# Six batches' queries and keys, transposed ahead of time and kept in DRAM

## Chip, cores, metric

The kernel runs on one core of a Trainium2 chip. The metric is the time on the device of one execution, in microseconds (us). The core's engines work in parallel, each through its own list of instructions in order: PE (TensorE, the matrix engine, which also transposes by a matmul with an identity matrix), DVE (VectorE), ACT (ScalarE), POOL (GpSimd). SP issues nearly all DMA transfers, in order as well. PE writes its results to PSUM, and another engine copies them to SBUF.

## What is computed

Attention over the 32 largest scores of each query, then a Fourier mixing block with a two-layer network. The inputs are float32: q, k and v of 8 batches, 8 heads, 576 tokens, 64 channels.

```python
scores = scale * np.matmul(q, k.transpose(0, 1, 3, 2))
kth = np.partition(scores, -top_k, axis=-1)[..., -top_k:-top_k + 1]
scores = np.where(scores >= kth, scores, -1000000000.0)
attn = np.exp(scores - np.max(scores, axis=-1, keepdims=True))
attn = attn / (np.sum(attn, axis=-1, keepdims=True) + 1e-09)
x = np.matmul(attn, v)                   # then (B, H, S, D) -> (B, S, H*D)
mixed = np.real(np.fft.fft(np.fft.fft(x, axis=1), axis=2))
u = x + mixed
un = (u - mean(u)) / np.sqrt(var(u) + 1e-06)
out = u + np.maximum(un @ w_ch1, 0.0) @ w_ch2
```

## The kernel before

**Work and steps.** Two heads make a pair: 4 pairs a batch, 32 in all. Tokens are cut into four blocks of 128 and a tail of 64. An item is one block of queries of one head (or the tails of both heads together): 9 items a pair, 36 a batch, 288 in all. The main loop at the end of the kernel makes one step per item, and each step appends instructions to every engine's list. The order on each engine is therefore written out by the program: a dictionary `plan` holds functions under a step and a place (`at(step, where, fn)`), and the step runs the places in a fixed order.

**What an item passes through.** PE multiplies q and k (`scores`, L401, L386, and L371 for the tail of the keys), ACT copies the scores to SBUF as S (L404, L393, L375), three steps ahead of DVE. DVE takes the 32 largest by four times MAX8 (L425) with MATCH_REPLACE8 between (L427). POOL makes the bounds nt (L434), ACT the mask (L448), POOL subtracts it (L451), ACT takes the exponential (L459). In the first batch, PE then transposes the probabilities (`transposes`, L527, L538, L542), ACT copies them to PT (L530 and after), and PE multiplies them with v (`attend`, L564). In later batches the transposes go through DRAM planes and a transposing DMA instead (`plane`, L472, L485; `turn`, L506).

**Preparing q and k.** The scores need q and k with the channels on partitions. SP loads them with the tokens on partitions (`load_nat`, `load_half`, `load_tails`), in pieces of 256 bytes a token. `prep` (L308 on PE) transposes five blocks of the pair, with two PSUM buffers of the pool `ps_t`, and ACT copies the result: for q a copy of 512 columns and one of 64 (L316), for k one of 512 (L318) and two for the tail, into a tile of its own, kt (L322). The loop calls it for the next pair, for q in the first step of a pair, for k in the sixth.

**The first batch is special.** In it there is no work of the network yet. Instead, the weights are converted: the inputs hold them as 64-bit floats, 32 chunks are loaded (L187), and ACT (L192, L208, L211, at the place "convert", the first thing of ACT's step), DVE (L200) and POOL (L219, L221) make float32 of them, about one chunk a step up to step 35. In a step of this batch ACT has, in order: the conversions, the exp of the last item, copies of scores, copies of `prep`, copies of PT, and the mask of the present item. PE has: scores, `prep`, the transposes of the last item, the product with v (in four steps of nine), three with 128 columns and one with 192.

**Later batches.** The mixing (`dft_tokens`, `dft_channels`) and the network of a batch (`mlp_units`: L966, L993, L1032, L1163) run on PE while the next batch's items pass. The function `level` spreads those units over the steps by estimated cost; `fixed_cost` gives a step's own PE work, with 0.7 us for each `prep`. After the last item there remain the mixing and the network of the last batch.

Of the kernel before, what the change touches and what calls it, by code (L numbers as in the profile page):

```python
# [9 lines left out]
F32 = mybir.dt.float32  # L10
# [9 lines left out]
P = 128  # L20
TH = 32
# [52 lines left out]
def kernel(  # L74
# [9 lines left out]
    nc = tc.nc  # L84
    B, H, S, D = q.shape
    DM = H * D
# [59 lines left out]
    cc = const.tile([P, 2], F32, name="cc", tag="cc")  # L146
    nat_t = const.tile([P, NC, 2, D], F32, name="nat", tag="nat")

    kt_t = const.tile([P, P], F32, name="kt", tag="kt")

    ftail = const.tile([P, DM + 1], F32, name="ftail", tag="ftail")
    v_t = [const.tile([P, NC, 2, D], F32, name=f"v{i}", tag=f"v{i}") for i in range(2)]

# [68 lines left out]


    nat, qT_of, kT_of, v_of, PT, Ssb, Wk, Wp, M8, Nt = ({} for _ in range(10))
    x_of, o_of, xT_of, rd_of = ({} for _ in range(4))


# [6 lines left out]

    def load_half(dst, src, pair, e, h, queue=None):

        r0 = h * (HS if src is q else 2 * P)
        (queue or nc.sync).dma_start(  # L240
            out=dst[:, 2 * h:2 * h + 2, e, :],
            in_=head_of(src, pair, e)[r0:r0 + 2 * P].rearrange("(t p) d -> p t d", p=P),
        )

    def load_tails(dst, src, pair, queue=None, heads=(0, 1)):
        for e in heads:
            if src is q:
                for h in range(2):
                    (queue or nc.sync).dma_start(
                        out=dst[TH * h:TH * (h + 1), NF, e, :],  # L250
                        in_=head_of(src, pair, e)[HS * h + 2 * P:HS * (h + 1)],
                    )
            else:
                r0 = TAIL * e if src is v else 0
                (queue or nc.sync).dma_start(
                    out=dst[r0:r0 + TAIL, NF, e, :], in_=head_of(src, pair, e)[NF * P:S]
                )

    def load_nat(n, pair):
        if pair < NPAIR:  # L260
            nat[n, pair] = nat_t
            src = q if n == "q" else k
            b, hp = divmod(pair, NPB)
            both = src[b, 2 * hp:2 * hp + 2]
            if n == "k":
                for e in range(2):
                    nc.sync.dma_start(
                        out=nat_t[:, 0:NF, e, :],
                        in_=both[e, 0:NF * P].rearrange("(c p) d -> p c d", p=P),
                    )  # L270
                nc.sync.dma_start(
                    out=nat_t[0:TAIL, NF, :, :], in_=both[:, NF * P:S].rearrange("e r d -> r e d")
                )
                return
            for e in range(2):
                for h in range(2):
                    load_half(nat_t, src, pair, e, h)
            for h in range(2):
                nc.sync.dma_start(
                    out=nat_t[TH * h:TH * (h + 1), NF, :, :],  # L280
                    in_=both[:, HS * h + 2 * P:HS * (h + 1)].rearrange("e r d -> r e d"),
                )

    def load_v(pair):
        if pair < NPAIR:
            v_of[pair] = v_t[pair % 2]
            for e in range(2):
                nc.sync.dma_start(
                    out=v_of[pair][:, 0:NF, e, :],
                    in_=head_of(v, pair, e)[0:NF * P].rearrange("(c p) d -> p c d", p=P),  # L290
                )
            load_tails(v_of[pair], v, pair)

    def prep(n, pair, blocks=((0, NF), (NF, NC))):

        if pair >= NPAIR:
            return 0.0
        src, got_of = nat[n, pair], qT_of if n == "q" else kT_of
        if pair not in got_of:
            got_of[pair] = attp.tile(  # L300
                [P, S if n == "q" else NF * P], F32, name=f"{n}T_{pair}", tag=f"{n}T",
                bufs=2 if n == "q" else 1
            )
        t_sb = got_of[pair]
        for c0, c1 in blocks:
            tp = ps_t.tile([P, 4, P], F32, name=f"tp{n}_{pair}_{c0}", tag="tp")
            for c in range(c0, c1):
                nc.tensor.transpose(  # L308
                    tp[:, c - c0, :], src[:, c, :, :].rearrange("p h d -> p (h d)"), ident
                )  # L310
            if c0 < NF:
                dst, got = t_sb[:, c0 * P:c1 * P], tp.rearrange("p a c -> p (a c)")[:, 0:(c1 - c0) * P]
            else:
                dst, got = t_sb[:, NF * P:], tp[:, 0, 0:TAIL]
            if n == "q":
                nc.scalar.mul(out=dst, in_=got, mul=scale)  # L316
            elif c0 < NF:
                nc.scalar.copy(out=dst, in_=got)  # L318
            else:
                for e in range(2):  # L320
                    r = slice(D * e, D * (e + 1))
                    nc.scalar.copy(out=kt_t[r, TAIL * e:TAIL * (e + 1)], in_=tp[r, 0, 0:TAIL])  # L322
        return 0.7


    IN_PAIR = [(0, 0), (0, 1), (1, 0), (1, 1), (4, None), (2, 0), (2, 1), (3, 0), (3, 1)]
# [7 lines left out]
    def scores(i, part):  # L334
# [3 lines left out]
        if not 0 <= i < N:  # L338
            return 0.0
        pair, t, e = items[i]  # L340
        qT, kT = qT_of[pair], kT_of[pair]
        rows = ROWS[t]
        if part == 0:
            for n in range(1 if e is None else 2):
# [210 lines left out]
    def attend(pair, ch, c0=0, c1=None):  # L555

        c1 = CW[ch] if c1 is None else c1
        pt, vv = PT[pair, ch], v_of[pair]
        if c0 == 0:
            o_of[pair, ch] = ps_o.tile([P, CW[0]], F32, name=f"o_{pair}_{ch}", tag="o")  # L560
        o = o_of[pair, ch]
        for c in range(NC):
            for e in range(2):
                nc.tensor.matmul(  # L564
                    o[D * e:D * (e + 1), c0:c1],
                    lhsT=vv[:, c, e, :],
                    rhs=pt[:, NF if c == NF else (NF + 1) * e + c, c0:c1],
                    start=(c == 0),
                    stop=(c == NC - 1),
                )  # L570
        return (c1 - c0) / 115.0
# [699 lines left out]
    kn0 = batp.tile([P, NC, 2, D], F32, name="kn0", tag="y")  # L1271
    for t in (kn0, nat_t):
        nc.vector.memset(t[TAIL:P, NF, :, :], 0.0)
    nc.vector.memset(kt_t, 0.0)

    nat["q", 0], nat["k", 0] = nat_t, kn0
    nc.scalar.dma_start(out=ident, in_=id_d.ap())
    for e in range(2):
        load_half(nat_t, q, 0, e, 0)
    for e in range(2):  # L1280
        load_half(kn0, k, 0, e, 1, nc.scalar)
        load_half(kn0, k, 0, e, 0)
    load_tails(kn0, k, 0, queue=nc.scalar, heads=(0,))
    load_tails(kn0, k, 0, heads=(1,))
    for e in range(2):
        load_half(nat_t, q, 0, e, 1)
    load_tails(nat_t, q, 0)
    nc.scalar.activation(out=warm, in_=cc[:, 0:1], func=AF.Exp)
    nc.vector.memset(cc[:, 1:2], FAR)
    for t in mv + den_t:  # L1290
        nc.vector.memset(t, 1.0)
    for t in v_t:
        nc.gpsimd.memset(t[TAIL:P, NF, 0, :], 0.0)
        nc.gpsimd.memset(t[0:TAIL, NF, 1, :], 0.0)
    nc.gpsimd.memset(ftail, 0.0)
    prep("q", 0, ((0, 2),))
    prep("k", 0)
# [30 lines left out]
    for n, s0 in enumerate(start_of):  # L1328
        at(s0 + 1, "convert", lambda n=n: scale_high(n))
        at(s0 + 1, "convert", lambda n=n: rest(n))  # L1330
        at(s0 + 1, "shift", lambda n=n: shift(n))
        at(s0 + 1, "join", lambda n=n: join(n, 0))
        at(s0 + 1, "pool", lambda n=n: join(n, 1))
        at(s0 + 1, "load", lambda n=n: load(n + AHEAD))

    ones = batp.tile([P, P], F32, name="ones", tag="yt")
    nc.vector.memset(ones, 1.0 / DM)
# [120 lines left out]
    def fixed_cost(i):  # L1458

        t = 0.55 if 0 <= i - 2 < N and not by_dma(i - 2) else 0.0  # L1460
        if i + 3 < N:
            t += {0: 1.04, 1: 0.3, None: 0.9}[items[i + 3][2]]
            if by_dma(i + 3) and items[i + 3][2] is not None:
                t += -0.3 if items[i + 3][2] else 0.3
        ch = chunk_at(i)[1] if i > PER_BATCH + 3 else {4: 0, 8: 1}.get((i - 3) % PER_PAIR)
        t += 0.0 if ch is None else (CW[ch] / 115.0 + 0.14 * len(CHUNKS[ch]))
        if i < N and i % PER_PAIR in (0, 5):
            t += 0.7
        return t + costs.get(i, 0.0)

# [27 lines left out]
    while i < N + 5 or plan or queue or sums:  # L1498
# [13 lines left out]
        preps = []  # L1512

        q_step = i == 2 if pair_of == 0 else i % PER_PAIR == 0
        if i < N and q_step:
            preps.append(lambda: prep("q", pair_of + 1))
        if i < N and i % PER_PAIR == 5:
            preps.append(lambda: prep("k", pair_of + 1))
        last_scores = []
        if PER_BATCH < j < N and j % PER_PAIR == 0 and by_dma(j):  # L1520
            fixed.append(lambda: 0.0)
# [30 lines left out]
        if short:  # L1552
# [2 lines left out]
            piece = {1: (0, 0, P), 4: (0, P, CW[0]), 6: (1, 0, P), 8: (1, P, CW[1])}.get(r)  # L1555
            if piece is not None:
                fixed.append(lambda: attend(pair, *piece))
            if i == PER_BATCH:
                fixed.append(lambda: attended(NPB - 1, 1, late_next) or 0.0)
                fixed.append(lambda: to_tokens(NPB - 1, 1, False))  # L1560
# [9 lines left out]
            mask(i - 1)  # L1570
        plane(i - 2, 0)
        plane(i - 2, 1)
        run(i, "convert")
        if short:
            expo(i - 1)
# [28 lines left out]
        if i < N:  # L1604
            if q_step:
                load_nat("k", pair_of + 1)
            if i % PER_PAIR == 5:
                load_nat("q", pair_of + 2)
            if i % PER_PAIR == 7:
# [64 lines left out]
```

## Time and profile before

| what | value |
|---|---|
| median of 3 runs | 1843.72 us (1843.49 to 1846.41) |
| the profiled execution | 1843.5 us, of which span 1841.7 us |
| PE busy | 1683.0 us (91%) |
| DVE busy | 1540.8 us (84%) |
| ACT busy | 1295.2 us (70%) |
| POOL busy | 919.1 us (50%) |
| DMA packets | 513504, of them under 512 bytes 398288 |
| transposes of q and k on PE (L308) | 320, in 64 groups of five |

The span is the time from the first to the last instruction. In the prediction, a view by stretch gives, for each window of time, its length and the busy time of each engine in it (x the number of instructions), then the mean clock granted to PE as a share of full speed, the busy share of the 16 DMA engines and what they moved. PEld is the weight load of PE, beside PE. A line of waits reads: engine, what it wrote and its line, who it waited for, total us, times, longest. A line of a timeline reads: start, duration, engine, line, operation, out<-in, shapes, count, and in brackets the idle time before it with what ended it. Matmuls overlap, so that the distance between two starts says more than a duration.

### The profile page before, as it was taken

To read this page: it belongs to the slowest core of one execution; us is meant where nothing else is said; L and a number is where in the kernel's file an instruction comes from. 1 tells how busy PE (TensorE), PEld (TensorE's weight loads), DVE (VectorE), ACT (ScalarE), POOL (GpSimd) and SP (SyncE) were. 2 spreads that over 40 slices of the span, in tenths; PEclk is the share of its full clock that TensorE was granted. 3 is DMA by queue.
4 is the path that set the end of the run, shared out by engine and by line. 5 is a ranking of instruction groups with operands and counts; after the bars stand their busy time and mean duration, and the time that the engine had idled before them with its cause. 6 is when DMAs were issued, how large, how long until landed. Compare 5 with 4: busy or idle time off the path is not lost.

```text
span 1841.7 us, 26992 instructions
## 1 busy us (share of the span) xinstructions
PE 1683.0 (91%) x8134; PEld 1082.6 (59%) x8134; DVE 1540.8 (84%) x3301; ACT 1295.2 (70%) x3104; POOL 919.1 (50%) x1286
## 2 busy tenths in 40 slices
PE   5677699899899998999999999999999899999998
PEld 3344465365555755667565656576566656686677
DVE  8999989899899999989899899999998889834010
ACT  6979658787788878877887779777887678642100
POOL 4868744546735466355644665356635555250012
PEclk7777899999999999999999999999999999999999
DMA  5333016752458855586556845595557745520051
GB/s 168 108 99 112 20 44 159 203 141 64 127 136 210 212 129 141 141 217 177 116 143 175 210 115 150 141 253 133 134 134 204 177 110 139 144 81 7 6 174 57
DMA packets 513504, 249.16 MB, mean 135 GB/s; under 512 B 398288, under 2 KB 502352, under 8 KB 513360
## 3 DMA queue, kind: packets, MB, share of 16 engines
q1 hardware_dynamic: 511440, 243.04, 51.3%
q0 software_dynamic: 1152, 4.19, 0.7%
q8 instruction: 65, 1.06, 0.2%
q14 instruction: 79, 0.65, 0.1%
q10 hardware_dynamic: 768, 0.21, 0.0%
HBM read 93.63 MB, written 84.74 MB: 97 GB/s over the span
## 4 chain that ended last, share of the span: by engine, by line
PE 45%; POOL 8%; ACT 6%; issue 5%; DMA 2%; DVE 2%; SPq 0%; POOLq 0%; DVEq 0%; ACTq 0%
PE hp L966 18%; PE o L564 4%; PE cw L1163 4%; PE cp L993 4%; POOL wk L451 4%; PE sp L401 3%; PE cv L1163 3%; PE cp L1032 2%; ACT wk L448 2%; POOL fg L651 2%; DMA PT<-planes 1%; PE mp L816 1%; PE sp_t L371 1%; ACT wk L472 1%; DVE m L425 1%
## 5 line engine op out<-in xcount | busy, mean ns | idle before, releaser
L451 POOL TENSOR_TENSOR wk<-S,wk 128x576 f32<-128x576 f32 x288 | 407.7, 1415 | 515.3 <-ACT wk L448 506.4
L425 DVE MAX8 m<-wk 128x8 f32<-128x576 f32 x864 | 618.5, 742 | 0.1
L966 PE MATMUL hp<-unT,w 128*128 128x256 f32 (+1 forms) x2048 | 524.3, 408 | 2.9 <-ACT hT L970 2.1
L966 PEld LDWEIGHTS hp<-unT,w 128*128 128x128 f32 x2048 | 379.3, 191 | 106.5 <-issue 10.1
L427 DVE MATCH_REPLACE8 wk<-m,wk 128x576 f32<-128x576 f32 x576 | 425.9, 739 | 0.0
L472 ACT COPY wk<-S 128x576 uint16<-128x576 uint16 x468 | 289.5, 670 | 0.0
L448 ACT ACTIVATE wk<-S,nt 128x576 f32<-128x576 f32 x288 | 223.5, 776 | 79.7 <-POOL nt L434 78.4
L993 PE MATMUL cp<-w,hT 128*128 128x512 f32 x512 | 231.8, 593 | 0.0
L425 DVE MAX8 m<-S 128x8 f32<-128x576 f32 x288 | 214.8, 746 | 18.5 <-ACT S L375 17.5
L970 ACT ACTIVATE hT<-hp 128x320 f32<-128x320 f32 (+1 forms) x256 | 103.8, 412 | 178.8 <-PE hp L966 177.3
L564 PE MATMUL o<-PT,v 128*64 128x256 f32 (+3 forms) x1440 | 199.5, 422 | 24.5 <-DMA PT<-planes 19.7
L427 DVE MATCH_REPLACE8 wk<-m,S 128x576 f32<-128x576 f32 x288 | 213.0, 740 | 0.0
L459 ACT ACTIVATE S<-wk,nt 128x576 f32<-128x576 f32 x234 | 184.2, 787 | 24.5 <-POOL wk L451 23.3
L401 PE MATMUL sp<-kT,qT 64*128 64x512 f32 (+1 forms) x528 | 167.2, 663 | 9.3 <-ACT means L1357 5.7
L564 PEld LDWEIGHTS o<-PT,v 128*64 128x64 f32 x1440 | 115.7, 156 | 100.9 <-issue 31.0
L404 ACT COPY S<-sp 128x512 f32<-128x512 f32 (+1 forms) x264 | 141.9, 588 | 31.8 <-PE sp L401 30.5
L993 PEld LDWEIGHTS cp<-w,hT 128*128 128x128 f32 x512 | 93.1, 191 | 89.2 <-issue 88.4
L1108 POOL TENSOR_TENSOR hT<-hT 128x512 f32<-128x512 f32 x64 | 81.2, 1275 | 117.7 <-ACT hT L970 87.6
L434 POOL TENSOR_TENSOR nt<-m,cc 128x2 f32<-128x2 f32 x288 | 59.4, 206 | 139.9 <-DVE m L425 138.1
L1163 PE MATMUL cw<-w,hT 128*128 128x256 f32 x448 | 105.6, 386 | 11.5 <-ACT ct L1133 10.2
L371 PEld LDWEIGHTS sp_t<-kt,qT 128*128 128x128 f32 x320 | 51.3, 195 | 103.2 <-issue 68.9
L1163 PEld LDWEIGHTS cw<-w,hT 128*128 128x128 f32 x448 | 83.6, 193 | 27.4 <-ACT ct L1133 12.6
(161 smaller groups left out, 2135.7 us busy)
## 6 DMA issues: line engine op xcount, KB each, us to landing
planes<-wk SPq DMA_DIRECT2D x208, 288.0 KB, 2.7
w<-w_parts SPq DMA_DIRECT2D x82, 512.0 KB, 4.9
space<-in_moe_w_ch_dram SPq DMA_DIRECT2D x32, 512.0 KB, 3.6
nat<-in_q_dram SPq DMA_DIRECT2D x128, 64.0 KB, 2.3
v<-in_v_dram SPq DMA_DIRECT2D x64, 128.0 KB, 2.9
out_dram<-x SPq DMA_DIRECT2D x32, 256.0 KB, 2.7
nat<-in_k_dram SPq DMA_DIRECT2D x62, 128.0 KB, 3.1
planes<-wk SPq DMA_DIRECT2D x52, 144.0 KB, 2.7
```

Of the source, the lines that this page charges most:

```text
L401: nc.tensor.matmul(sp[r], lhsT=qT[hd, q_cols], rhs=kT[hd, :], start=True, stop=True)
L404: nc.scalar.copy(out=s_t[r, keys], in_=sp[r])
L425: ops.append(lambda src=src, m8=m8: nc.vector.max(out=m8, in_=src))
L427: ops.append(lambda src=src, m8=m8: nc.vector.match_replace(w, m8, src, NEG))
L448: nc.scalar.activation(out=w, in_=Ssb[i], func=AF.Relu, scale=-FAR, bias=Nt[i][:, 1:2])
L451: nc.gpsimd.tensor_tensor(out=w, in0=Ssb[i], in1=w, op=ALU.subtract)
L459: nc.scalar.activation(out=Ssb[i] if by_dma(i) else w, in_=w, func=AF.Exp, bias=Nt.pop(i)[:, 0:1], accum_out=den_t[pair % 3][:, c:c + 1],)
L472: nc.scalar.copy(out=words[:, half, :], in_=src[:, half, :])
L564: nc.tensor.matmul(o[D * e:D * (e + 1), c0:c1], lhsT=vv[:, c, e, :], rhs=pt[:, NF if c == NF else (NF + 1) * e + c, c0:c1], start=(c == 0) ...
L966: nc.tensor.matmul(hp[:, 0:w], lhsT=w1[:, dt, P * it:P * (it + 1)], rhs=unT[:, dt, 0:w], start=(dt == 0), stop=(dt == NDT - 1),)
L993: nc.tensor.matmul(cp, lhsT=hT[:, it, P * n:P * (n + 1)], rhs=w2[:, it, :], start=(it == 0), stop=(it == NIT - 1),)
L1163: nc.tensor.matmul(dst, lhsT=h()[a][:, kc, :], rhs=rhs_of(kc), start=start and kc == 0, stop=kc == NK - 1, skip_group_check=True,)
```

## The change

Three things are changed.

**q and k ahead.** For pairs 8 to 31 (the last six batches) `prep` is no longer called. In its place, jobs run in the first batch: one for each of these 24 pairs (`ahead`) and one for the tails of each of the six batches (`tails_ahead`), 30 jobs at the steps 3 + 32n // 30. A job loads the tokens two steps before its step; in its step PE transposes them, after the product with v; at the start of ACT's next step (place "fetch", ahead of "convert") ACT copies the result from two PSUM banks back over the staging tile; two steps after its step SP stores it to the DRAM tiles `q_made` and `k_made`. The staging tiles borrow the buffers of x, y and fold_s. Later, `load_made` loads a pair's q and k, ready transposed, with one DMA each, a pair ahead. The buffer of k is now one of two in turn, `keys_t` and the old `nat_t`, with the tail behind the 512 columns. `fixed_cost` leaves out the 0.7 us for these pairs.

**Four keys to a partition.** Keys 4p to 4p + 3 are loaded to partition p, for k and for v alike, so that a load reads 1 KB runs. The order of the keys in the scores changes with it; the tail stays apart.

**v in one load.** v of a pair is laid out by head, and its first 512 keys come by one DMA for both heads instead of two; the tails still by one each.

```diff
+    def load_made(n, pair):
+        if not AHEAD_FROM <= pair < NPAIR:
+            return
+        b, hp = divmod(pair, NPB)
+        if n == "q":
+            qT_of[pair] = attp.tile([P, S], F32, name=f"qT_{pair}", tag="qT", bufs=2)
+            nc.sync.dma_start(out=qT_of[pair], in_=q_made[b][:, hp, :])
+        else:
+            kT_of[pair] = keys_t if pair % 2 else nat_keys
+            nc.sync.dma_start(out=kT_of[pair], in_=k_made[b][:, hp, :])
...
     def load_v(pair):
         if pair < NPAIR:
             v_of[pair] = v_t[pair % 2]
+            b, hp = divmod(pair, NPB)
+            nc.sync.dma_start(
+                out=v_of[pair][:, :, 0:NF, :].rearrange("p e c d -> p e (c d)"),
+                in_=v[b, 2 * hp:2 * hp + 2, 0:NF * P].rearrange("e (p c) d -> p e (c d)", c=NF),
+            )
             for e in range(2):
                 nc.sync.dma_start(
-                    out=v_of[pair][:, 0:NF, e, :],
-                    in_=head_of(v, pair, e)[0:NF * P].rearrange("(c p) d -> p c d", p=P),
+                    out=v_of[pair][TAIL * e:TAIL * (e + 1), e, NF, :],
+                    in_=head_of(v, pair, e)[NF * P:S],
                 )
-            load_tails(v_of[pair], v, pair)
...
     def prep(n, pair, blocks=((0, NF), (NF, NC))):
 
-        if pair >= NPAIR:
+        if pair >= AHEAD_FROM:
             return 0.0
...
+    def ahead(pair, slot):
...
+        def load():
+            for e in range(2):
+                for h in range(2):
+                    load_half(tiles(0), q, pair, e, h)
+                load_k(tiles(1), pair, e)
+
+        def turn_them():
+            tps = []
+            for n in range(2):
+                tp = bank([P, NF, P], f"tpa_{pair}_{n}")
+                for c in range(NF):
+                    nc.tensor.transpose(
+                        tp[:, c, :], tiles(n)[:, c, :, :].rearrange("p h d -> p (h d)"), ident
+                    )
+                tps.append(tp)
+
+            def fetch():
+                for n, tp in enumerate(tps):
+                    dst, got = stages[slot][:, n, :], tp.rearrange("p a c -> p (a c)")
+                    if n == 0:
+                        nc.scalar.mul(out=dst, in_=got, mul=scale)
+                    else:
+                        nc.scalar.copy(out=dst, in_=got)
+            return fetch
+
+        def store():
+            nc.sync.dma_start(out=q_made[b][:, hp, 0:NF * P], in_=stages[slot][:, 0, :])
+            nc.sync.dma_start(out=k_made[b][:, hp, 0:NF * P], in_=stages[slot][:, 1, :])
...
+    def job(step, made):
+        load_it, turn_it, store_it = made
+        at(step - 2, "load", load_it)
+        at(step, "pe_ahead", lambda: at(now[0] + 1, "fetch", turn_it()))
+        at(step + 2, "load", store_it)
+
+    stage_tiles()
+    jobs = []
+    for b in range(AHEAD_FROM // NPB, B):
+        jobs.append(lambda b=b: tails_ahead(b))
+        for n in range(NPB * (b - 2), NPB * (b - 1)):
+            jobs.append(lambda n=n: ahead(AHEAD_FROM + n, n % len(stages)))
+    for n, made in enumerate(jobs):
+        job(3 + 32 * n // len(jobs), made())
...
             if piece is not None:
                 fixed.append(lambda: attend(pair, *piece))
+            fixed.append(lambda: run(i, "pe_ahead") or 0.0)
...
         plane(i - 2, 0)
         plane(i - 2, 1)
+        run(i, "fetch")
         run(i, "convert")
...
         if i < N:
             if q_step:
                 load_nat("k", pair_of + 1)
+                load_made("q", pair_of + 1)
+            if i % PER_PAIR == 1:
+                load_made("k", pair_of + 1)
```

`tails_ahead` does the same for the 64 last tokens of q and k of the eight heads of a batch: four transposes, one copy of 256 columns and two of 64 partitions by 256 columns, and two stores.

## Prediction

> **What bounds the kernel now.** I read four views in this order: the busy time of the engines by stretch, the waits of ACT in the first batch, the order of time in that batch, and the order of time on PE later on.
>
> ```profile
> core 0: us, PE busy (x) PEld busy (x) DVE busy (x) ACT busy (x) POOL busy (x), PEclk, DMA share, GB/s
> 20.00:215.00 195.00, 128.17 (x644) 81.03 (x645) 191.65 (x396) 163.82 (x383) 149.54 (x141) 0.76 0.33 97
> 240.00:280.00 40.00, 39.08 (x208) 28.04 (x207) 32.42 (x70) 23.05 (x57) 19.34 (x33) 0.99 0.19 49
> 320.00:360.00 40.00, 32.05 (x118) 14.56 (x119) 31.80 (x68) 30.02 (x73) 22.36 (x29) 0.92 0.77 206
> 500.00:690.00 190.00, 180.97 (x884) 114.88 (x882) 188.11 (x403) 155.59 (x372) 97.20 (x140) 0.98 0.68 170
> 690.00:1560.00 870.00, 838.52 (x4132) 535.11 (x4129) 802.55 (x1718) 682.85 (x1622) 453.88 (x680) 1.00 0.63 158
> ```
>
> The first row is the first batch: DVE is busy 98% and sets the pace, PE has room (66%), and ACT, at 84%, has 31 us left. From 500 to 690 DVE is full again (99%). From 690 to 1560 PE is the fullest (96%, DVE 92%). So PE time saved counts in the last stretch, and PE time added counts least in the first. But the work that is moved has an ACT half too, and in the first batch ACT is the engine to look at. Its waits there, from 20 to 215 us:
>
> ```profile
> ACT PT L530 <- PE tpP L527: 14.1, 22, 1.0
> ACT S L404 <- PE sp L401: 6.2, 9, 1.1
> ACT wk L459 <- POOL wk L451: 5.8, 9, 1.5
> ACT S L375 <- PE sp_t L371: 3.2, 2, 2.9
> ACT wk L448 <- POOL nt L434: 1.0, 2, 0.6
> ```
>
> The reader is to see the last line: ACT waited for DVE's result (through nt) for only 1.0 us. Its idle time is not room in front of DVE; it is short turns to PE and POOL inside its own chain. ACT runs as long as DVE does, by chance almost equal.
>
> **What is saved later.** Pairs 8 to 31 lose both preparations: 48 times 5 transposes on PE. Their price where PE is full:
>
> ```profile
> 818.41 0.71 PE L308 MATMUL tpq<-ident,nat 128*128 128x128 f32 x5
> 818.95 1.25 PE L1163 MATMUL cv<-w,hT 128*128 128x256 f32 x5
> ```
>
> Start to start 0.54 us for five (the 0.71 overlaps what follows). In the timeline 35 of the 48 start after 690: 35 x 0.54 = 18.9 us. Eight lie between 500 and 690, where DVE covers them: 0, at most 8 x 0.54 = 4.3. Five lie before 500, where PE was busy 108.16 of 120 us: half of 5 x 0.54, 1.4 (0 to 2.7). From 380 to 1600 the preparations' weight loads waited for ACT's S copies, with which they share PSUM buffers, 8.1 (q) and 6.0 us (k). Taken away, that wait is gone, or moves to the next matmul that needs ACT: 0 to 14.1; in the timeline about two thirds of it lie before 690, mostly under DVE's pace, so I take a third, 4.7. Saved: 18.9 + 1.4 + 4.7 = 25.0, at most 40. If the 96% of PE is itself held by chains through ACT and DMA, only half of the 18.9 comes: at least 9.5. ACT's copies that go too (24 x 1.8 us) lie beside a fuller PE and count nothing by themselves.
>
> **What is added in the first batch.** 30 jobs, one in each step from 3 to 33 but 18: 24 with 8 transposes and two copies 128x512 from PSUM, 6 with 4 transposes, one copy 128x256 and two 64x256. Two copies of 128x512 take ACT 1.07 us (S<-sp, the row at 109.17 us), the small ones 0.39 (xT) and 0.37 (S<-sp 64x256): 24 x 1.07 + 6 x 1.13 = 32.5 us. ACT's work becomes 163.8 + 32.5 = 196.3 in a stretch of 195. Of its waits, those for tpP and sp_t stay (the turn exp, transposes, copy is unchanged): 17.3. Those for sp, POOL and nt (13.0) I let vanish, since PE and POOL get ahead while ACT copies. That is 213.6, so +18.6: ACT takes the pace over from DVE.
>
> Then the place of the copies. They stand on ACT after the mask and before the three conversions and the next exp; the transposes stand on PE behind the product with v. The order of time, PE and then ACT:
>
> ```profile
> 104.87 0.42 PE L538 MATMUL tpP_t<-ident,wk 128*128 128x128 f32 x1
> 105.22 2.86 PE L564 MATMUL o<-PT,v 128*64 128x128 f32 x20
> 108.01 1.13 PE L401 MATMUL sp<-kT,qT 64*128 64x512 f32 x4
> 109.07 0.66 PE L527 MATMUL tpP<-ident,wk 128*128 128x128 f32 x4
> ```
> ```profile
> 105.60 0.27 ACT L539 COPY PT<-tpP_t 128x128 f32<-128x128 f32 x1
> 105.75 0.79 ACT L448 ACTIVATE wk<-S,nt 128x576 f32<-128x576 f32 x1
> 108.06 0.78 ACT L459 ACTIVATE wk<-wk,nt 128x576 f32<-128x576 f32 x1 [1.52 <-POOL wk L451]
> ```
>
> The product ends at 108.0; four transposes take 0.66, so the first copy could start at 108.7, but ACT is done with its mask at 106.5: it waits 2.2 us, and behind it stand the conversions, the exp and, after them, the S copies on which DVE lives three steps later. Where the product has 192 columns it starts at 93.44, the next matmul at 97.11, and the mask ends at 95.14: 97.11 + 0.66 - 95.14 = 2.6. Jobs meet a product in 12 steps (5, 14, 23 and 32 with 192 columns; 7, 9, 11, 16, 20, 25, 27 and 29 with 128): 4 x 2.6 + 8 x 2.2 = 28.0 us. In the other steps the transposes follow the tpP group directly and are done before the mask: 0.
>
> First batch: 18.6 + 28.0 = +46.6. Bounds: all waits absorbed, 196.3 - 195 = +1.3; all 31.2 kept and the stalls on top, 196.3 + 31.2 + 28.0 - 195 = +60.5. I take the value between, as the turn through PE can't vanish. PE itself gains 24 x 8 + 6 x 4 = 216 transposes of about 0.14 us at clock 0.76 (0.54 / 5 / 0.76), 31 us, against 67 idle: covered, but for the stalls just counted.
>
> The clock: with 159 us of PE work in some 241 us the busy share stays at 66%, for which the first row shows 0.76 (0.92 at 80%, 0.99 at 98%); I keep 0.76. The Trainium skill's page "TensorE: Matmul & The Clock Gate" (section "Part 1: The HAM clock gate") says that the clock is halved by default and that activity inside short windows frees it, not the mean share; the jobs fill gaps, so by it the clock could go to 1.00, a product and its four transposes would shrink from 3.5 to 2.7 us, and the sum would be some 10 us less. No row shows that for this batch.
>
> **Costed at nothing.** DMA: some 28 MB more (24 pairs of 0.5 MB and the tails, in and out) over 241 us is 117 GB/s on 78; the row at 320 moved 206 GB/s at a share of 0.77. SP: eight issues more a step at 0.47 us (median of the q loads) is 3.8 us of a step of 5.6, behind the load of weights, which waits for POOL; a job's loads are issued two steps ahead (11 us) and land in 2.5 us (at most 5.6). Later, the loads of the made q and k stand five steps ahead of their scores; uncovered, a landing a pair would cost 24 x 2.5 = 60 us. The buffers that the jobs borrow from x and y are stored from by step 35 and written anew from step 37 on: one landing, if that were too early. The order of the keys and v's single load change no engine's work.
>
> **The sum.** 1841.7 + 46.6 - 25.0 = 1863.3 of span; the profiled run had 1.8 around its span (1843.5), and the median is 0.2 above that: 1865 us.
>
> **Rivals.**
> 1. Faster: ACT's copies do fit. What decides is ACT's wait at the copies behind the product. If ACT comes to its mask later against PE than I think, or PE's clock rises, the transposes are ready, the 31.2 us of waits take up the 32.5, and the first batch grows by some 10 us: 1843.7 + 10 - 25 = 1829. Faster begins where the growth stays under 25 - 3.7. For it: PE's 34% idle. Against: nt's 1.0 us, and the fixed order on PE.
> 2. The saving does not come: behind 690 DVE is at 92%, and the waits of other lines grow where the preparations were. 1843.7 + 46.6 - 9.5 = 1881. Against: PE is full at 96%.
> 3. Loads late: SP stood 126 us in 27 waits for POOL at the weights' loads in this batch; eight issues queue behind each. Late by 2 us in 24 jobs, PE stands in order, and so does ACT: 1865 + 48 = 1913. Against: two steps of lead.
>
> **Chances.** The forecast 0.60, rival 1 0.18, rival 2 0.15, rival 3 0.07. By 0.2% (3.7 us, what a measurement of this kernel can tell): faster 0.18 (rival 1), same 0.06 (the low end of the forecast, growth near 25), slower 0.76. The extremes are 1843.7 + 1.3 - 40 = 1805 and 1843.7 + 60.5 - 9.5 = 1895; leaving out most of rival 1, rival 3 and the ends, 1832 to 1890. The forecast's own range is 1848 to 1882.
>
> **What would show it.** In the first batch: its end some 45 us later, ACT over 90% busy with waits of 2 us at the new copies for the job's transposes, DVE waiting for S and for the converted weights, the clock near 0.76. Later: no transposes of q and k from pair 8 on, a batch between 900 and 1500 about 4 to 5 us shorter (eight times 0.54), PE still above 94%. It is wrong if DVE keeps 98% in the first batch, or if the later batches gain more than 45 us together.

## Result, and the profile after

| | before | after |
|---|---|---|
| median | 1844.47 us (1843.49 to 1846.41, 4 runs) | 1870.31 us (1867.37 to 1873.03, 4 runs) |
| profiled execution, span | 1841.7 us | 1865.6 us |

The change makes the kernel slower: ratio 1.0138, 95% interval 1.012 to 1.0157. The forecast was 1865 us, in a range of 1832 to 1890.

Where did the time go? POOL makes one nt per item, right behind DVE, so the starts of these instructions cut the trace into batches. Times in us, from the first item of a batch to that of the next:

| | first batch | second | third and fourth | fifth to seventh, mean | first item of the last batch at | end of span |
|---|---|---|---|---|---|---|
| before | 201.7 | 217.0 | 384.8 | 201.1 | 1424.0 | 1841.7 |
| after | 254.5 | 213.5 | 387.9 | 194.9 | 1458.0 | 1865.6 |

The first batch is 52.8 us longer. The second is 3.5 shorter, the third and fourth together 3.1 longer, each of the next three 6.2 shorter, and the last, with what follows it, 10.1 (417.7 to 407.6). By its first item the second batch is 53.1 us late, by the end of the span 23.9 of that are left: 29.2 us were saved.

The view by stretch of the changed kernel (window, length, busy time of PE, PEld, DVE, ACT, POOL, clock, DMA share, GB/s):

```profile
20.00:215.00 195.00, 127.96 (x677) 92.53 (x677) 156.60 (x314) 152.88 (x353) 113.54 (x109) 0.77 0.74 194
20.00:265.00 245.00, 160.62 (x843) 114.23 (x845) 194.36 (x394) 193.07 (x447) 146.00 (x139) 0.77 0.73 193
690.00:1560.00 870.00, 843.00 (x4100) 529.16 (x4099) 832.77 (x1784) 680.80 (x1589) 479.06 (x710) 1.00 0.63 164
```

In the window from 20 to 215 us DVE was busy for 191.65 before and is for 156.60 now: it has lost the pace. The second row is about the same work in its new length. No engine is full in it, PE 66%, DVE 79%, ACT 79%. Where the time goes, the waits from 20 to 265 us tell, first of ACT, then of DVE:

```profile
ACT PT L646 <- PE tpP L643: 15.1, 20, 1.4
ACT stage_x L430 <- PE tpa L421: 13.1, 5, 3.1
ACT stage_y L430 <- PE tpa L421: 13.1, 6, 3.0
ACT S L491 <- PE sp_t L487: 3.2, 2, 3.0
ACT S L520 <- PE sp L517: 2.3, 3, 0.9
ACT stage_tails L388 <- PE tpt L383: 2.2, 1, 2.2
ACT wk L575 <- POOL wk L567: 0.5, 1, 0.5
ACT stage_x L432 <- PE tpa L421: 0.5, 2, 0.3
ACT stage_y L432 <- PE tpa L421: 0.3, 1, 0.3
```
```profile
DVE w L200 <- ACT w L192: 46.2, 20, 4.7
DVE m L541 <- ACT S L491: 3.6, 4, 1.0
```

ACT's work (193.1) and ACT's waits (their sum is 50.3) fill 243.4 of 245 us, and none of these waits is for DVE. Work and waits filled ACT's time before as well (163.8 + 30.3 of 195); what is new is that DVE no longer keeps up beside it. So ACT's list, with its turns to PE, is taken for the bound; e4 and e5 below test it. DVE shows where it feels that: 46.2 us at the converted weights (L200, 2.4 us before), whose first conversion on ACT (L192) now stands behind the new copies. Of ACT's waits, 29.2 us are at the copies of the jobs (stage). One of them in order of time, on PE and then on ACT:

```profile
114.80 3.01 PE L680 MATMUL o<-PT,v 128*64 128x192 f32 x20 [0.25 <-ACT PT L646]
117.74 1.09 PE L421 MATMUL tpa<-ident,stage_x 128*128 128x128 f32 x8
```
```profile
115.72 0.77 ACT L564 ACTIVATE wk<-S,nt 128x576 f32<-128x576 f32 x1
118.44 0.60 ACT L430 ACTIVATE stage_x<-tpa 128x512 f32<-128x512 f32 x1 [1.95 <-PE tpa L421]
118.93 0.58 ACT L432 COPY stage_x<-tpa 128x512 f32<-128x512 f32 x1
119.40 0.68 ACT L192 ACTIVATE w<-space 128x512 f32<-128x512 f32 x1
121.07 0.79 ACT L575 ACTIVATE wk<-wk,nt 128x576 f32<-128x576 f32 x1
```

ACT is done with its mask at 116.5. PE is still at the product with v until 117.7 and then transposes; the first copy starts at 118.4. The conversions and the exp, which stand behind it on ACT, come later by that.

### The profile page after: what moved, and what is told of

Read it like the earlier page. It is cut to its first block, busy times and chain, and to the rows that moved or that the text cites. A ratio compares the mean times of both kernels' runs of the same rounds, so it can differ in the third digit from the quotient of the medians.

```text
span 1865.6 us, 26973 instructions
## 1 busy us (share of the span) xinstructions
PE 1690.3 (91%) x8110; PEld 1088.2 (58%) x8110; DVE 1545.0 (83%) x3301; ACT 1291.9 (69%) x3050; POOL 916.8 (49%) x1287
## 4 chain that ended last, share of the span: by engine, by line
PE 55%; DVE 17%; ACT 11%; POOL 5%; issue 5%; DMA 4%; SPq 2%; POOLq 0%; DVEq 0%; ACTq 0%
PE hp L1082 19%; PE cp L1109 8%; DVE m L541 8%; DVE wk L543 8%; PE o L680 6%; PE sp L517 4%; PE cw L1279 3%; PE yp L871 3%; PE cv L1279 2%; POOL wk L567 2%; PE sp_t L487 2%; ACT wk L564 2%; DMA planes<-wk 1%; ACT wk L588 1%; PE cp L1148 1%
## 5 line engine op out<-in xcount | busy, mean ns | idle before, releaser
L517 PE MATMUL sp<-keys,qT 64*128 64x512 f32 (+1 forms) x336 | 107.8, 682 | 11.8 <-ACT means L1486 7.6
L643 PE MATMUL tpP<-ident,wk 128*128 128x128 f32 x216 | 42.4, 330 | 72.6 <-ACT wk L575 48.9
L1279 PE MATMUL cv<-w,hT 128*128 128x256 f32 x384 | 90.7, 388 | 10.0 <-issue 5.7
```

The costliest lines, as they stand in the source:

```text
L517: nc.tensor.matmul(sp[r], lhsT=qT[hd, q_cols], rhs=kT[hd, :], start=True, stop=True)
L1279: nc.tensor.matmul(dst, lhsT=h()[a][:, kc, :], rhs=rhs_of(kc), start=start and kc == 0, stop=kc == NK - 1, skip_group_check=True,)
```

## The experiments

Each was timed beside the kernel before on the same chip. The table gives the median, the ratio to the kernel before with its 95% interval, and the trace's first batch and later batches as above; the sections say what each is for.

| | median us | ratio | first batch | fifth to seventh, mean |
|---|---|---|---|---|
| the change | 1870.3 | 1.0138 (1.012 to 1.0157) | 254.5 | 194.9 |
| e1 jobs only | 1893.8 | 1.0255 (1.0208 to 1.0302) | 253.7 | 202.3 |
| e2 saving only | 1821.0 | 0.9859 (0.981 to 0.9909) | 202.8 | 195.5 |
| e3 layout only | 1843.0 | 0.9973 (0.9951 to 0.9994) | 202.9 | 200.4 |
| e4 copies later | 1843.7 | 0.9973 (0.9954 to 0.9992) | 225.0 | 197.1 |
| e5 transposes first | 1847.6 | 1.0006 (0.9988 to 1.0024) | 228.3 | 195.2 |
| e6 loads and stores only | 1817.9 | 0.9856 (0.9835 to 0.9877) | 202.7 | 195.5 |
| e7 e4, 16 pairs | 1829.4 | 0.9907 (0.9892 to 0.9922) | 217.1 | 195.1 |
| e8 e7, weights' loads behind | 1827.9 | 0.9902 (0.9885 to 0.9919) | 217.0 | 194.4 |
| e9 no copies | 1832.8 | 0.9926 (0.9908 to 0.9944) | 219.4 | 195.1 |
| e10 e7, transposes first | 1828.1 | 0.9903 (0.9886 to 0.992) | 213.3 | 194.9 |

### e1, e2, e3: the change taken apart

e1 runs the jobs but lets all pairs be prepared as before (the jobs and the made tiles count from JOBS_FROM):

```diff
-    AHEAD_FROM = 2 * NPB
+    AHEAD_FROM, JOBS_FROM = NPAIR, 2 * NPB
```

> The jobs run in the first batch as in the change and store their results, but nobody reads them: all pairs are prepared as before. Theory A (the first batch pays for ACT's added copies and for their place behind the product with v): the whole cost without the saving, 53 us over before, near 1897 us, the first batch as long as in the change. Theory B (the change costs little in the first batch, and the later batches are what became slower): below 1860 us. Theory C (it is the made q and k read back that disturb the later batches): well below the change, as nothing is read back.

e2 has no jobs; the later loads of q (and of k likewise) take equal amounts from the inputs:

```diff
-    for n, made in enumerate(jobs):
-        job(3 + 32 * n // len(jobs), made())
...
-            nc.sync.dma_start(out=qT_of[pair], in_=q_made[b][:, hp, :])
+            nc.sync.dma_start(out=qT_of[pair], in_=q[b, 2 * hp:2 * hp + 2].rearrange("e (x t) d -> (e x) (t d)", x=P // 2))
```

> No jobs: from pair 8 on q and k are loaded, with the same shapes and sizes, straight from the inputs as if they were stored transposed. This leaves out the transposing of the last six batches, so the values are not the reference's; top-k takes the same instructions for any values. Theory A: the saving alone, 25 to 29 us under before, near 1817 us, the first batch as before. Theory B: the saving is not there, 1835 to 1850 us. e1 and e2 should add up to the change.

e3 has neither jobs nor made q and k:

```diff
-    AHEAD_FROM = 2 * NPB
+    AHEAD_FROM = NPAIR
```

> No jobs and all pairs prepared as before: what remains is four keys to a partition, 1 KB runs, k of one tile and v in one load. Theory A: no engine's work changes, within 3 us of before, 1841 to 1848 us. If the layout has a part in the loss or the gain, it is further away.

All three came out as theory A had it; e3, inside its 1841 to 1848, lies 3.9 us under the kernel before that was timed beside it (1846.95). The jobs cost 2.55%, the saving brings 1.41%, and 1.0255 x 0.9859 = 1.011. Both hold the new layout, which this product counts twice; divided by e3's 0.9973 it is 1.0138, the change's own ratio, nearer than the intervals would let one ask. Of the three, the first batch is long only in e1, which has the jobs. The layout alone is 0.06 to 0.5% faster, so it has no part in the loss, but it has one in the gain. Theories B and C fall: the later batches did become shorter, and e1, which reads nothing back, is not faster than the change but slower.

### e4: ACT's copies after the exp

```diff
-        run(i, "fetch")
         run(i, "convert")
         if short:
             expo(i - 1)
+        run(i, "fetch")
```

> The change, with one line moved: ACT's copies of the transposed blocks come after the conversions and the exp, not before them. Theory A: conversions (1.7 us) and exp (0.95 us) cover the 2.2 to 2.6 us for which the copies waited for PE, so the 28 us of stalls go, DVE no longer waits for the converted weights, and the copies cover part of ACT's wait for the transposed probabilities: 1870 - 28 - 12 = 1830 us, at most 1842. Theory D (ACT's amount of work, not the place, sets the first batch): 1860 to 1870 us. Theory E (the DMA traffic or SP's queue sets it): no change, 1870 us.

Two lines changed places, and the first batch fell from 254.5 to 225.0: 29.5 us, where 28 had been worked out for the stalls and 29.2 measured. So it is the place of the copies, not their number, that makes the change a loss, and neither theory D nor theory E explains it as a whole. But 1830 was too hopeful: the time is 1843.7, above even the 1842 set as the most, and 23.3 us of the growth stay. What is left shows in the waits from 20 to 240 us, of ACT and then of PE:

```profile
ACT PT L646 <- PE tpP L643: 7.8, 11, 1.1
ACT S L520 <- PE sp L517: 5.6, 9, 1.1
ACT wk L575 <- POOL wk L567: 4.6, 3, 1.5
```
```profile
PE tpt L383 <- DMA stage_tails<-in_k_dram: 7.0, 3, 2.8
PE tpa L421 <- DMA stage_y<-in_q_dram: 4.0, 3, 2.4
PE tpa L421 <- DMA stage_x<-in_q_dram: 1.5, 1, 1.5
```

ACT's wait for the transposed probabilities is halved, as expected, but the waits for scores and POOL came back. And the staged tokens are now late for PE by 12.5 us, which they were not in the change. Shorter steps alone don't explain that: e5, with a first batch nearly as short, has 1.3 us of such waits. The cause stays open.

### e5: transposes ahead of the product

```diff
+            fixed.append(lambda: run(i, "pe_ahead") or 0.0)
             if piece is not None:
                 fixed.append(lambda: attend(pair, *piece))
-            fixed.append(lambda: run(i, "pe_ahead") or 0.0)
```

> The change, with the job's transposes put before the product with v on PE instead of behind it; ACT's copies stay where the change has them. Theory A: the transposes follow the tpP group at once and are ready before ACT's mask ends, so the 28 us of waits at the copies go and the time is near that of e4, 1840 to 1848 us; what is left over before is ACT's 32 us of copies. Theory F (e4 gained because the conversions came earlier for DVE and POOL, and the wait for PE is of no weight): 1860 to 1870 us.

The other end of the same wait. With ACT's copies left where the change has them, its waits at the copies fall from 29.2 to 2.1 us and the first batch to 228.3. Theory F, with its 1860 to 1870 us, falls. DVE still waits for converted weights, but for 16.1 us instead of 46.2. What is left of the growth, 26.6 us, goes with ACT's amount of work: from the first item to that of the second batch it is busy for 198.7 us, against 168.9 in the kernel before, and waits 2.6 us less (31.6 against 34.2).

### e6, e9: the job's parts

e6 keeps the jobs' loads and stores, e9 their transposes too; neither copies (both clear the rest of the tails' tile once, on POOL):

```diff
# e6
-        at(step, "pe_ahead", lambda: at(now[0] + 1, "fetch", turn_it()))
# e9
-        at(step, "pe_ahead", lambda: at(now[0] + 1, "fetch", turn_it()))
+        at(step, "pe_ahead", lambda: turn_it() and None)
```

> The change with the jobs' loads and stores, but without their transposes on PE and copies on ACT (that part is left out, so q and k of the last six batches are stored as they came and the values are not the reference's). Theory A: the 28 MB and SP's issues are hidden, the time is that of the saving alone, 1817 to 1823 us. Theory E (traffic or SP's queue costs): 1835 us or more; each us over 1821 is theirs.

> The change with the jobs' loads, transposes and stores, but without ACT's copies of the result (that part is left out, so the values are not the reference's). Theory A: without the copies nothing on ACT waits for PE and its work is that of before; PE's 216 transposes lie in its idle time, so the time is near e6 and e2, 1817 to 1826 us, the first batch under 206 us. Theory H (the transposes themselves delay the scores and the probabilities behind them on PE): 1835 us or more.

e6 is the saving alone to within 4 us (1817.9 against 1821.0): in e6 the 28 MB cost nothing that can be measured. The view by stretch of e6:

```profile
20.00:215.00 195.00, 126.47 (x641) 80.80 (x643) 191.91 (x395) 164.14 (x383) 149.42 (x141) 0.76 0.88 228
```

The DMA engines are 88% busy, and DVE does what it did before (191.91 against 191.65).

e9 is a miss, between the two theories. With the transposes the first batch is 16.7 us longer than in e6 (219.4 against 202.7), where they had been held to be covered. The waits in e9 from 20 to 225 us, of ACT and then of PE:

```profile
ACT S L520 <- PE sp L517: 16.5, 9, 2.8
ACT PT L646 <- PE tpP L643: 12.4, 16, 1.5
ACT S L491 <- PE sp_t L487: 10.1, 5, 3.0
```
```profile
PE tpa L421 <- DMA stage_y<-in_q_dram: 6.6, 6, 2.4
PE tpt L383 <- DMA stage_tails<-in_k_dram: 4.4, 2, 2.2
PE tpa L421 <- DMA stage_x<-in_q_dram: 2.9, 4, 1.1
```

ACT, which no longer stops at the copies, stops at the scores: 26.6 us, against 9.4 in the kernel before. Two things hold these up on PE. The transposes stand behind the product, and the next step's scores behind them: the copy of scores at 107.66 us waits 1.99 us with no late load ahead of it. And PE waits for staged tokens, 14.9 us in all with two smaller lines: the copy at 94.31 us waits 2.29 us behind two such waits. What each costs, no run tells.

### e7, e8, e10: jobs for the last four batches alone

The third and fourth batch gained nothing from the change, so their pairs need no job. e7 is e4 with

```diff
-    AHEAD_FROM = 2 * NPB
+    AHEAD_FROM = 4 * NPB
...
-        for n in range(NPB * (b - 2), NPB * (b - 1)):
+        for n in range(NPB * b - AHEAD_FROM, NPB * (b + 1) - AHEAD_FROM):
```

> e4 with the jobs for the last four batches alone (pairs 16 to 31, 20 jobs). Theory A: batches 2 and 3 are set by DVE and gained nothing from the change (197.8 and 190.1 us against 193.3 and 191.5), so the saving stays near 24 us, and with a third of the jobs gone the first batch grows by 15 us or less instead of 23: 1830 to 1838 us. Theory G (each pair's job costs and saves alike): no better than e4, 1843 us.

e8 puts the weights' loads into a later place of SP's step (`"load"` becomes `"load2"`), e10 is e7 with the edit of e5:

> e7 with the loads of weights issued behind the jobs' loads and stores in SP's step, so that these no longer stand behind a wait for POOL. Theory A: PE waited for staged tokens 12.5 us in e4's first batch because of that; with two thirds of the jobs some 8 us, which go in part: 2 to 8 us under e7. If late loads were not on the path: equal to e7. If the weights then come late: above e7.

> e7 with the transposes also put before the product with v on PE. Theory A: in e7 ACT hardly waits at the copies any more (1.6 us), so that the order on PE has nothing left to win, within 3 us of e7; it may lose a little where the product, put later, holds up the scores behind it.

e7 took 1829.4 us, 0.93% less than the kernel before and just under the range expected, and in each batch it did about what was expected: a first batch of 217.1 (15.4 longer, where 15 or less had been expected), the third and fourth at 387.9 as in the change, the later ones at 195.1. Theory G falls. e8 and e10 are not told apart from e7. e8 did not test what it was made for: in e7 the staged tokens were late by 0.5 us only, so there was nothing left to win. Whether it would help e4, with its 12.5 us, wasn't tried.

## Why the prediction was right, and where it was off

**The bound of the first batch.** Right. That ACT's idle time was no room in front of DVE was read from one line (nt, 1.0 us), and ACT did become the pacer.

**ACT's work, +18.6 us.** Nearly right. 196.3 us had been worked out, 193.1 were counted from 20 to 265 us. In the same window, the waits that were to stay, 17.3, measured 18.3; of the 13.0 that were to vanish, 2.8 stayed. "ACT over 90% busy" in the signs to look for was wrong, and not by the chip: the sum itself has 196 of 241.6, 81%. What is full is ACT's work together with its turns to PE.

**The stalls behind the product, 28.0 us.** Right: 29.2 in the trace, 29.5 by e4, and e5 removes them from the other side. DVE was to feel it at S and at the converted weights; it was the weights, 46.2 us, with 3.6 at S.

**The first batch, +46.6.** 52.8 measured. Over the whole batch, from its first item to that of the second, ACT's work grew by 30.0 us (168.9 to 198.9), less than the 32.5 of the sum, and the waits at the copies were 29.2 instead of 28.0. The term that was off is the one for waits that vanish, 13.0: those for scores, POOL and nt fell by 7.6 (16.9 to 9.3), while the one for the transposed probabilities grew by 1.0.

**PE's half, "covered, but for the stalls just counted".** It holds for the change, where ACT's waits for scores are shorter than before (5.5 us against 9.4). In e9, without the copies, the same transposes and the late tokens before them cost 16.7 us. A sum of the parts taken one by one (1.0 by e6, 16.7 by e9) and the rest (35.1 for the copies) therefore holds only in this order.

**The clock.** 0.77 in the first batch, at a busy share of 66%, as the row of before had it (0.76). The Trainium skill's page "TensorE: Matmul & The Clock Gate", section "Part 1: The HAM clock gate", has activity inside short windows free the clock, by which filled gaps could have brought it to 1.00; no run shows that for this batch. Nor does the busy share alone settle it: from 20 to 240 us e4 had 0.81 with PE busy for 154.85 of 220 us, e7 0.76 with 156.39.

**The saving, 25.0 us.** 29.2 measured. The stretch where DVE leads gave 0, as said. Each batch of the PE stretch became 6.2 us shorter, where eight times 0.54 made 4.3. From the first item of the fifth batch to that of the last, before and then after, the stretch and two of PE's waits in it:

```profile
820.70:1424.00 603.30, 586.50 (x2893) 375.75 (x2892) 558.94 (x1194) 473.44 (x1125) 314.67 (x467) 1.00 0.64 161
PE o L564 <- DMA PT<-planes: 7.0, 3, 3.9
PE tpu L881 <- ACT us L833: 1.1, 3, 0.4
```
```profile
873.40:1458.00 584.60, 571.31 (x2778) 361.65 (x2776) 556.39 (x1191) 456.70 (x1065) 316.17 (x468) 1.00 0.64 166
PE tpu L997 <- ACT us L949: 5.0, 3, 1.7
PE o L680 <- DMA PT<-planes: 0.2, 1, 0.2
```

Of the 18.7 us, 15.2 are PE's busy time, where 24 preparations at 0.54 make 13.0; e1 and e3, which both keep the preparations, differ there by 3.9, so the two are not told apart. The rest is waiting, 13.0 us instead of 16.9: the product's wait for transposed planes went, which had not been in the sum at all, and the one at tpu grew. The wait that was in the sum, 4.7 for the preparations' turns to ACT, is not in this stretch, neither before nor after. It did go (12.7 to 1.3 us from 280 to 1620 us), but others grew in its place (tpu from 2.4 to 8.4, yp from 2.3 to 8.1), and all of PE's waits in that window make 65.9 us before and 65.6 after. So that term was not too small; in the sum of the waits it brought nothing that can be seen. Why the planes come earlier was not settled; in the same stretch e1, without the saving, has 6.1 us of that wait, e3 3.6, and e2, with the saving, none.

The layout had been put at nothing, and e3 has it 0.06 to 0.5% faster, 1 to 9 us. With the layout in both kernels, e3 to e2 and e1 to the change, the ratios give 1.1 to 1.2%, some 21 us, for the preparations alone. The intervals are as wide as the difference, but part of the 29.2 may well be the layout's. That the total came within 6 us of the forecast is in part luck: the first batch cost 6.2 us more and the saving was 4.2 us larger than forecast, and the two offset each other.

**The rivals.** Rival 1 failed at the place that it named, the copies behind the product. e4 and e5 each remove that wait by one edit, and even so the first batch grew by 23.3 and 26.6 us, not by the 10 that rival 1 had: ACT's waits didn't take up the copies. Rival 2 fell with e2. Rival 3 fell for the change with its trace, where the only wait of PE put down to a job's tokens in the first batch is 0.2 us. In other orders of the same work tokens do come late, by 12.5 us in e4 and 14.9 in e9. The jobs' loads landed in 3.0 to 5.1 us in the change (medians), not in 2.5.

## What to carry to other kernels

Work that is moved into a stage "with room" has a half on every engine that it passes, and the half that decides may be the small one: here PE had 34% room and ACT had little, though it was idle for 16%: in e5, with the stalls gone, 29.8 us more of its work made the batch 26.6 us longer. Idle time that is made of turns to another engine is not room; look for whom the engine waits. And two engines in strict order hold each other up at the place where one list's long instruction (a product) stands before what the other list's next instruction needs: moving the reader behind work that doesn't need it, or the writer before the long instruction, made the first batch 26 to 30 us shorter here without removing anything. Move only what pays: a third of the pairs belonged to batches that another engine paced.

## What the runs showed of the hardware

The 16 DMA engines went from a share of 0.33 to 0.88 in the window from 20 to 215 us (97 to 228 GB/s, e6), while the busy time of DVE (191.65 to 191.91 us), ACT (163.82 to 164.14) and POOL (149.54 to 149.42) stayed as it was. What changed is the landing (medians, from issue): the weights' chunks of 512 KB took 4.6 us instead of 3.6. Pieces of 64 KB took 3.5 us before; in e6 those of `prep` took 2.3, the jobs' 3.5 to 3.9, and those of the tails 4.9.
